# A two-layer linear-attention and MLP kernel: token pieces of the second joint stage dealt to other slots, and four steps of the joint pairs in another order

## The chip, the cores and the metric

The kernel runs on one core of one Trainium2 chip. The metric is the device time of one execution in microseconds. The engines are named as in the profile: PE (TensorE, the matmuls), DVE (VectorE), ACT (ScalarE), POOL (GpSimd) and SP (SyncE, which here issues the DMAs).

## The reference

The input is x, 2048 tokens of 448 numbers. Twice in turn it goes through an attention block and an MLP block, each added to its own input:

```python
    x = A_x
    x = x + _A_ref(_layernorm(x, axis=-1), A_wqkv, A_wo)
    x = x + _B_ref(_layernorm(x, axis=-1), B_w1, B_b1, B_w2, B_b2)
    x = x + _A_ref(_layernorm(x, axis=-1), A_wqkv, A_wo)
    x = x + _B_ref(_layernorm(x, axis=-1), B_w1, B_b1, B_w2, B_b2)
```

`_A_ref` is linear attention with 16 heads of 28. `_B_ref`, where the change lies, is `gelu(x @ w1 + b1) @ w2 + b2` with an inner width of 1792. All is float32.

## The kernel before, in words

**Arithmetic.** Each float32 operand of a matmul is held as two fp32r tiles, a high part (a cast on ACT) and a low part (the operand less its high part, on DVE). A product is made of three matmuls, high by high, low by high and high by low, so a matmul with a low part waits for a DVE subtraction. In the names an h or l at the end stands for these parts: `gh` and `gl` are the parts of a gelu's output, `XH` and `XL` those of the tokens.

**Blocks and slices.** The tokens are taken in four blocks of 512, the inner width in 14 slices of 128. A slice's first product (hp, hx, hy, hz) makes 128 x 512 values for a block, gelu follows on ACT, and `mlp2` (L1269) multiplies slice i of a block by w2 and adds it into four banks y, one for each 128 tokens: twelve matmuls of 448 columns. When a block's last slice is through, `mlp2` adds the banks to the block's rows on DVE (L1300, four operations) and SP stores them.

**Stages of a layer.** After attention, `classic` (L1407) does slices 0 to 9 of blocks 0 and 1 one by one. The two `joint` pairs (L1444, k = 0 and 1) do slices 10 to 13 for both blocks at once, and `eight` (L1553) does all seven pairs of slices for blocks 2 and 3. `joint` and `eight` use a Strassen-like scheme: `product(k)` (L1184) takes a pair of slices and two blocks through seven products with sums of weight pieces and of token pieces. Products 1, 6, 7 and 4 add up in one bank hx, 5 and 3 in hy, 2 in hz. `keep` (L1202) copies a state of hx or hy to s1, s2 or s5 on ACT, DVE adds another bank to it (L1474, L1478, L1502, L1507, L1603, L1616, L1622), and `high` and `low` make gelu, gh and gl of it. `later` makes only the gelu and puts it by. Since product 4 goes on adding in hx, it must wait until s5's addition has read that bank.

**Between the stages.** `remainder` (L1522) ends block 1 and begins with the gelus of block 0 that were put by; `LATER = (11, 10, 13, 12)` is the order of their slices and `divide` (L1243) makes their gh and gl. Slices 11 and 10 go through `mlp2` in `remainder`, 13 and 12 in the first pair of `eight`, and 12 is block 0's last.

**Token pieces.** Before `eight` the tokens of blocks 2 and 3 come as A11, A12, A21 and A22, and the sums S1 to S4 are made of them. `token_sum` (L1162) adds two pieces, the first half (128 x 512) on POOL and the second on DVE, both on line L1165. `token_piece` (L1167) makes the high part of a half on ACT (L1170) and the low part on DVE (L1171). Product 1 needs A11, 2 needs A12, 5 S1, 6 S2, 7 S3, 3 S4 and 4 A22. S2 is written over A11, S3 over A21 and S4 over A12, so a sum may only be made when the piece below it has been split.

**What sets the order.** The schedule is manual: an engine runs its instructions in the order in which the code writes them, and waits where a semaphore is missing. The table `PLAN` (L1319) lists by slot what `behind(l, i, tr)` writes at place i: "sS30" is `token_sum` S3, half 0, "tA121" is `token_piece` A12, half 1, and "y02" loads rows of block 0. Slots 24 and 25 stand in `remainder`, slot 27 in the first pair of `eight`, 28 in joint pair 0. Beside all this, `make` (L491) writes the next steps by which ACT, POOL and DVE prepare the weight pieces of a coming pair (`sevens`, L452; lines L431 to L486).

Of the kernel before, what the change touches and what calls it, by code (L numbers as in the profile page):

```python
# [12 lines left out]
OP = mybir.AluOpType  # L13
# [9 lines left out]
def linear_attn_mlp_kernel(  # L23
# [12 lines left out]
    pe, act, dve, pool, sp = nc.tensor, nc.scalar, nc.vector, nc.gpsimd, nc.sync  # L36
# [454 lines left out]
    def make(n, steps=1):  # L491
        if n < len(ahead):
            if n not in makers:
                makers[n] = (sevens if ahead[n][1] == "x" else chunks)(n)
            for _ in range(steps):
                next(makers[n], None)
# [31 lines left out]
    def stage_a(l, t):  # L528
        sts[l, t] = ln_stats(xt.pop((l, t)))
# [637 lines left out]
    def token_piece(l, name, h, eng=dve):  # L1167
        x = view(l, name, h)
        hi, lo = (cols(placed(l, k, name, h)) for k in range(2))
        act.copy(hi, x)  # L1170
        eng.tensor_tensor(lo, x, f(hi), op=OP.subtract)  # L1171
# [63 lines left out]
    def divide_high(g):  # L1235
        gh = t512("A", 2, "gh", F32R)
        act.copy(gh, g)  # L1237
        return gh, t512("B", 2, "gl", F32R, APART)

    def divide_low(g, gh, gl):  # L1240
        dve.tensor_sub(gl, g, f(gh))  # L1241

    def divide(i, g):  # L1243
        gs[i] = divide_high(g)
        divide_low(g, *gs[i])
# [64 lines left out]
    def load_part(l, t):  # L1310
# [86 lines left out]
    LATER = (11, 10, 13, 12)  # L1397
# [4 lines left out]
    def first_pair(l, b):  # L1402
        return l * (2 * NP + NC) + FIRST[b]

    came = {}
# [38 lines left out]
    def joint(l, k, tr):  # L1444

        n = first_pair(l, "j") + k
        p = NC + k
        c = Pair(l, 0, p, n)

        def step():  # L1450
            make(n + 1)

        c.product(1)
        s1 = c.keep(c.X, "s1")
        if k:
            step()
            c.product(5)
            s5 = c.keep(c.Y, "s5")
            c.product(2)
            dve.tensor_tensor(s1, s1, c.Z, op=OP.add)  # L1460
            step()
            mlp2(l, 1, 2 * p - 1)
            c.product(6)
            s2 = c.keep(c.X, "s2")
            c.high(s1, 0)
            c.low(0)
            step()
            make(n)
            make(n + 2)
            step()  # L1470
            behind(l, 22, tr)
            step()
            c.product(3)
            dve.tensor_tensor(s2, s2, c.Y, op=OP.add)  # L1474
            c.high(s2, 1)
            step()
            c.product(7)
            dve.tensor_tensor(s5, c.X, s5, op=OP.add)  # L1478
            c.low(1)
            c.later(s5, 1)  # L1480
            step()
        else:
            behind(l, 20, tr)
            step()
            c.product(2)
            dve.tensor_tensor(s1, s1, c.Z, op=OP.add)
            make(n + 2)
            c.product(5)
            s5 = c.keep(c.Y, "s5")
            behind(l, 30, tr)  # L1490
            c.product(6)
            s2 = c.keep(c.X, "s2")
            c.high(s1, 0)
            c.low(0)
            behind(l, 26, tr)
            step()
            step()
            mlp2(l, 1, CUT - 1)
            make(n)
            c.product(7)  # L1500
            step()
            dve.tensor_tensor(s5, c.X, s5, op=OP.add)  # L1502
            c.later(s5, 1)
            step()
            behind(l, 28, tr)
            c.product(3)
            dve.tensor_tensor(s2, s2, c.Y, op=OP.add)  # L1507
            c.high(s2, 1)
            c.low(1)
            step()  # L1510
            behind(l, 21, tr)
        mlp2(l, 1, 2 * p)
        if k:
            divide(LATER[0], came.pop(LATER[0]))
            behind(l, 23, tr)
        c.product(4)
        c.later(c.X, 0)
        step()
        if k == 0:
            step()  # L1520
# [32 lines left out]
    def eight(l, k):  # L1553

        n = first_pair(l, 2) + k
        c = Pair(l, 2, k, n)
        onward = k == NP - 1 and l + 1 < LAYERS

        def step():
            if k < NP - 1:  # L1560
                make(n + 1)

        c.product(1)
        s1 = c.keep(c.X, "s1")
        if k:
            step()
            c.product(5)
            s5 = c.keep(c.Y, "s5")
            step()
            if onward:  # L1570
                stage_a(l + 1, 0)
            c.product(2)
            dve.tensor_tensor(s1, s1, c.Z, op=OP.add)
            c.high(s1, 0)
            step()
            c.product(6)
            s2 = c.keep(c.X, "s2")
            make(n)
            if k < NP - 2:
                make(n + 2)  # L1580
            step()
            mlp2(l, 2, 2 * k - 1)
            c.low(0)
            step()
            c.product(3)
            dve.tensor_tensor(s2, s2, c.Y, op=OP.add)  # L1586
            c.high(s2, 1)
            step()
            c.product(7)
            dve.tensor_tensor(s5, c.X, s5, op=OP.add)  # L1590
            c.low(1)
            c.later(s5, 1)
            step()
            beside(l, k)
            if onward:
                stage_a(l + 1, 1)
        else:
            mlp2(l, 0, LATER[2])
            behind(l, 27, None)
            c.product(2)  # L1600
            make(n + 2)
            divide(LATER[3], came.pop(LATER[3]))
            dve.tensor_tensor(s1, s1, c.Z, op=OP.add)  # L1603
            c.product(5)
            s5 = c.keep(c.Y, "s5")
            c.product(6)
            s2 = c.keep(c.X, "s2")
            c.high(s1, 0)
            c.low(0)
            make(n)  # L1610
            mlp2(l, 0, LATER[3])
            step()
            step()
            step()
            c.product(7)
            dve.tensor_tensor(s5, c.X, s5, op=OP.add)  # L1616
            for h in range(2):
                token_piece(l, "A22", h)
            c.later(s5, 1)
            step()  # L1620
            c.product(3)
            dve.tensor_tensor(s2, s2, c.Y, op=OP.add)  # L1622
            step()
            c.high(s2, 1)
            c.low(1)
            step()
        mlp2(l, 2, 2 * k)
        c.product(4)
        c.later(c.X, 0)
        step()  # L1630
        if k == 0:
            step()
# [82 lines left out]
    for l in range(LAYERS):  # L1715
# [35 lines left out]
        for k in range(NP - NC):  # L1751
            joint(l, k, tr)
        remainder(l, tr)
        for k in range(NP):
            eight(l, k)
# [29 lines left out]
```

## Time and profile before

| | us |
|---|---|
| median of 3 runs | 876.27 (874.73 to 876.62) |
| the profiled execution's own time | 875.26 |
| its span, first to last instruction | 873.5 |
| PE busy in the span | 848.5 (97%) |
| DVE, ACT, POOL busy | 617.3, 515.7, 404.7 |

A row of the timeline has the start in us from the span's start, the duration, the engine, the line, what is written and from what, and in brackets how long the engine sat idle before it and who released it. Rows of one kind that follow one another are put together (x2, x4). Matmuls overlap: the start of one to the start of the next says more than a duration. The changed places come once in each layer: in the first layer between about 264 and 320 us, in the second between 693 and 751 us.

### The profile page before, as it was taken

What the parts mean: (1) busy time and instruction counts of PE and PEld (TensorE: products, weight loads), DVE (VectorE), ACT (ScalarE), POOL (GpSimd) and SP (SyncE); (2) the same over time, 40 slices, a digit from 0 to 9 for tenths busy, and PEclk for the clock granted to TensorE, in tenths of its full rate; (3) what the DMA queues carried; (4) which work ended last, traced back from release to release, by engine and by line L of the source; (5) the groups of instructions that cost most, each with busy time, mean ns of one, the idle gap of its engine ahead of it and who ended that gap; (6) DMA issues with size and microseconds to landing.
All of it is one profiled execution on the core that took longest, in us unless ns stands there. A gap on an engine that the chain in (4) does not pass through costs nothing.

```text
span 873.5 us, 12572 instructions
## 1 busy us (share of the span) xinstructions
PE 848.5 (97%) x4065; PEld 751.1 (86%) x4065; DVE 617.3 (71%) x1086; ACT 515.7 (59%) x1069; POOL 404.7 (46%) x474
## 2 busy tenths in 40 slices
PE   9999999999999899999999999989999998999998
PEld 8899987878888688889999998878888877888897
DVE  7898597568967775466888977953898669536443
ACT  7666664564676576664446665636556765665531
POOL 3456533455557544750533333243665582544310
PEclk9999999999999999999999999999999999999999
DMA  5375757656564533437545444584655453332361
GB/s 169 125 252 180 232 141 236 203 174 205 191 217 131 177 113 118 146 97 250 203 155 191 149 128 127 188 260 154 221 178 205 140 169 127 106 110 76 112 229 43
DMA packets 104461, 144.75 MB, mean 166 GB/s; under 512 B 10188, under 2 KB 91468, under 8 KB 104396
## 3 DMA queue, kind: packets, MB, share of 16 engines
q1 hardware_dynamic: 102620, 141.52, 49.4%
q10 hardware_dynamic: 1776, 2.44, 0.9%
q8 instruction: 32, 0.52, 0.3%
q14 instruction: 33, 0.27, 0.1%
HBM read 88.68 MB, written 50.86 MB: 160 GB/s over the span
## 4 chain that ended last, share of the span: by engine, by line
PE 60%; DVE 15%; ACT 8%; DMA 8%; issue 5%; POOL 2%; SPq 1%; DVEq 0%; ACTq 0%; POOLq 0%
PE hx L1200 9%; PE G L731 7%; PE psk L389 6%; PE y L1297 6%; PE y L1296 6%; PE y L1295 6%; PE psq L389 5%; PE hy L1200 4%; DMA temp<-in_B_w_dram 2%; PE hz L1200 2%; PE hp L1264 2%; DVE gl L1241 2%; DMA sp<-sq_q 2%; DVE pq L990 1%; ACT xm L1078 1%
## 5 line engine op out<-in xcount | busy, mean ns | idle before, releaser
L1297 PE MATMUL y<-w2h,gl 128*128 128x448 f32 x447 | 162.5, 363 | 7.8 <-DVE gl L1241 7.6
L1296 PE MATMUL y<-w2l,gh 128*128 128x448 f32 x447 | 164.3, 368 | 0.0
L1295 PE MATMUL y<-w2h,gh 128*128 128x448 f32 x447 | 163.4, 365 | 0.2 <-ACT gh L1237 0.2
L1241 DVE TENSOR_TENSOR gl<-g,gh 128x512 fp32r<-128x512 f32 x84 | 74.2, 883 | 68.8 <-ACT gh L1237 68.7
L1297 PEld LDWEIGHTS y<-w2h,gl 128*128 128x128 f32 x447 | 84.6, 189 | 17.1 <-DVE gl L1241 11.7
L1295 PEld LDWEIGHTS y<-w2h,gh 128*128 128x128 f32 x447 | 84.4, 189 | 9.9 <-ACT gh L1237 0.7
L1296 PEld LDWEIGHTS y<-w2l,gh 128*128 128x128 f32 x447 | 84.6, 189 | 6.5
L1264 PE MATMUL hp<-XH,W 128*128 128x512 f32 x280 | 87.8, 390 | 0.2 <-ACT XH L371 0.2
L1215 ACT ACTIVATE g<-s,b1s 128x256 f32<-128x256 f32 x84 | 38.2, 502 | 55.5 <-DVE s L1586 34.9
L1057 POOL TENSOR_TENSOR brs<-bst,few 128x1 f32<-128x1 f32 x32 | 18.2, 570 | 102.3 <-ACT bst L1055 102.3
L389 PE MATMUL psk<-wk,XH 128*128 128x448 f32 x210 | 61.8, 364 | 0.0
L570 POOL TENSOR_TENSOR xnl<-x,xnh 128x384 fp32r<-128x384 f32 x32 | 35.4, 1107 | 55.7 <-ACT xnh L569 27.8
L1264 PE MATMUL hp<-XL,W 128*128 128x512 f32 x160 | 60.7, 391 | 0.6 <-DVE XL L372 0.6
L1264 PEld LDWEIGHTS hp<-XH,W 128*128 128x128 f32 x280 | 52.4, 188 | 10.0 <-ACT XH L371 0.6
L389 PE MATMUL psq<-wq,XH 128*128 128x448 f32 x196 | 57.2, 365 | 0.3 <-DVE eq L408 0.3
L1237 ACT CAST gh<-g 128x512 fp32r<-128x512 f32 x84 | 52.1, 621 | 3.0 <-PE y L1296 0.6
L968 POOL TENSOR_TENSOR pz<-pq,zb 128x448 f32<-128x448 f32 x26 | 31.0, 1193 | 45.0 <-DVE dn L979 33.9
L1266 ACT ACTIVATE g<-hp,b1s 128x512 f32<-128x512 f32 x40 | 27.3, 682 | 36.9 <-PE hp L1264 27.7
L213 POOL TENSOR_TENSOR brs<-bve,few 128x1 f32<-128x1 f32 x31 | 17.1, 550 | 66.7 <-DVE bve L212 61.4
L731 PE MATMUL G<-kh,xnh 128*128 128x448 f32 x128 | 46.7, 368 | 0.0
L1200 PE MATMUL hx<-XH,W 128*128 128x512 f32 x140 | 43.7, 391 | 2.8 <-DVE s L1478 2.8
L731 PE MATMUL G<-kl,xnh 128*128 128x448 f32 x128 | 46.1, 365 | 0.2 <-DVE kl L618 0.2
(275 smaller groups left out, 2276.8 us busy)
## 6 DMA issues: line engine op xcount, KB each, us to landing
temp<-in_B_w_dram SPq DMA_DIRECT2D x20, 384.0 KB
x<-in_A_x_dram SPq DMA_DIRECT2D x32, 224.0 KB
pq_d<-eq SPq DMA_DIRECT2D x32, 224.0 KB
pq<-pq_d SPq DMA_DIRECT2D x32, 224.0 KB
g_d<-g SPq DMA_DIRECT2D x28, 256.0 KB
x<-x_d SPq DMA_DIRECT2D x32, 224.0 KB
gb<-g_d SPq DMA_DIRECT2D x28, 256.0 KB
raw<-in_B_w_dram SPq DMA_DIRECT2D x18, 384.0 KB
```

What stands on the lines that cost most here:

```text
L389: pe.matmul(o, x, p, start=(i == 0), stop=(i == 10))
L570: pool.tensor_tensor(lo[:, :TL], xn[:, :TL], f(h[:, :TL]), op=OP.subtract)
L731: pe.matmul(acc[c], w, k, start=first and c not in others[0], stop=last and c not in others[1])
L968: pool.tensor_tensor(pz, pq, tr.zb, op=OP.mult)
L1200: pe.matmul(o, w, r, start=(k in (1, 5, 2) and i == 0), stop=(i == len(made) - 1), skip_group_check=True)
L1215: act.activation(g[:, s].rearrange("p (u i n) -> p i u n", u=2, i=4), x[:, s].rearrange("p (i u n) -> p i u n", u=2, i=4), AF.Gelu_apprx_t ...
L1237: act.copy(gh, g)
L1241: dve.tensor_sub(gl, g, f(gh))
L1264: pe.matmul(hp, w, r, start=(k == 0), stop=(k == len(made) - 1))
L1295: pe.matmul(acc[j], gh[:, s], hi, start=first, stop=False)
L1296: pe.matmul(acc[j], gh[:, s], lo, start=False, stop=False)
L1297: pe.matmul(acc[j], gl[:, s], hi, start=False, stop=stop)
```

## The change

In the slots, seven entries go to a later slot and two sums go up within theirs:

```diff
-        "sS11 tA111 tA120 tA121 tS10 sS30 sS20 sS31",
+        "sS11 tA111 sS30 sS20 tA120",
...
-        "tS30 tS31 tS40 tS41",
+        "tS20 tS21 sS40 sS41 tS30 tS31 tS40 tS41",
```

Slot 25 is now "tA121 tS10 tS11 sS31 sS21" and the loads, where it was "tS11 sS21 tS20 tS21 sS40 sS41" and the loads. So the second half of A12, the first of S1 and a sum go from slot 24 to slot 25, and S2's pieces and S4's sums from 25 to 27.

In joint pair 1, the gelu of s2 and a step of the weights are written behind product 7 and s5's addition:

```diff
             c.product(3)
             dve.tensor_tensor(s2, s2, c.Y, op=OP.add)
-            c.high(s2, 1)
-            step()
             c.product(7)
             dve.tensor_tensor(s5, c.X, s5, op=OP.add)
+            c.high(s2, 1)
+            step()
             c.low(1)
```

In joint pair 0, `mlp2` of slice 10 of block 1 is written ahead of product 3 (it stood behind it, ahead of product 4):

```diff
             behind(l, 28, tr)
+            mlp2(l, 1, 2 * p)
             c.product(3)
...
-        mlp2(l, 1, 2 * p)
         if k:
+            mlp2(l, 1, 2 * p)
             divide(LATER[0], came.pop(LATER[0]))
```

In the first pair of `eight`, `divide` of slice 12 goes ahead of slot 27, and `mlp2` of slice 12, with the four additions of block 0's rows that it ends in, ahead of `low` of s1:

```diff
             mlp2(l, 0, LATER[2])
+            divide(LATER[3], came.pop(LATER[3]))
             behind(l, 27, None)
             c.product(2)
             make(n + 2)
-            divide(LATER[3], came.pop(LATER[3]))
             dve.tensor_tensor(s1, s1, c.Z, op=OP.add)
...
             c.high(s1, 0)
+            mlp2(l, 0, LATER[3])
             c.low(0)
             make(n)
-            mlp2(l, 0, LATER[3])
```

What this does to the engines' queues, all in the first layer: PE in joint pair 0, where product 3 (hy from S4) is taken out between product 7 (hx from S) and `mlp2` of slice 10:

```order
 L1200 MATMUL hx<-S_2837,W_130 128x512 x2
 L1200 MATMUL hx<-S_2838,W_130 128x512
-L1200 MATMUL hy<-S_3074,W_130 128x512 x2
-L1200 MATMUL hy<-S_3075,W_130 128x512
-L1200 MATMUL hy<-S_3074,W_130 128x512
-L1200 MATMUL hy<-S_3075,W_130 128x512
 L1295 MATMUL y_2371<-w2h,gh 128x448
 L1296 MATMUL y_2371<-w2l,gh 128x448
```

and put in behind that, right ahead of product 4 (hx from XH):

```order
 L1296 MATMUL y_2374<-w2l,gh 128x448
 L1297 MATMUL y_2374<-w2h,gl 128x448
+L1200 MATMUL hy<-S_3074,W_130 128x512 x2
+L1200 MATMUL hy<-S_3075,W_130 128x512
+L1200 MATMUL hy<-S_3074,W_130 128x512
+L1200 MATMUL hy<-S_3075,W_130 128x512
 L1200 MATMUL hx<-XH,W_130 128x512 x2
 L1200 MATMUL hx<-XL,W_130 128x512
```

Five matmuls went behind twelve. DVE in `remainder` before, from the second half of A11; the gl here is that of slice 13, and the L1165 rows are sums:

```order
L1171 TENSOR_TENSOR XL_129<-sp_3239,XH_128 128x2x256
L1171 TENSOR_TENSOR XL_129<-sp_3072,A12_3325 128x2x256
L1171 TENSOR_TENSOR XL_129<-sp_3239,A12_3325 128x2x256
L1171 TENSOR_TENSOR S1_3330<-S1_3286,XH_128 128x2x256
L1165 TENSOR_TENSOR sp_3241<-sp_3239,sp_3241 128x2x4x64
L1241 TENSOR_TENSOR gl_3354<-g_3266,gh_3352 128x512
```

and after, until gl of slice 12 (the second gl):

```order
L1171 TENSOR_TENSOR XL_129<-sp_3239,XH_128 128x2x256
L1171 TENSOR_TENSOR XL_129<-sp_3072,A12_3327 128x2x256
L1241 TENSOR_TENSOR gl_3348<-g_3266,gh_3346 128x512
L1171 TENSOR_TENSOR XL_129<-sp_3239,A12_3327 128x2x256
L1171 TENSOR_TENSOR S1_3352<-S1_3286,XH_128 128x2x256 x2
L1165 TENSOR_TENSOR sp_3241<-sp_3239,sp_3241 128x2x4x64
L1165 TENSOR_TENSOR sp_3239<-S1_3286,sp_3239 128x2x4x64
L1241 TENSOR_TENSOR gl_3402<-g_3293,gh_3400 128x512
```

gl of slice 13 has moved ahead of the second half of A12, the first half of S1 and a sum. DVE further on in the first pair of `eight`, before, from gl of slice 12 and s1's addition; the second gl is that of s1, slice 0 of blocks 2 and 3:

```order
L1241 TENSOR_TENSOR gl_3428<-g_3293,gh_3426 128x512
L1603 TENSOR_TENSOR s1_3394<-s1_3394,hz_3417 128x512
L1241 TENSOR_TENSOR gl_3453<-g_3448,gh_3451 128x512
L486 TENSOR_TENSOR W1_130<-raw_3046,W1_130 64x128
L1300 TENSOR_TENSOR r0_0_3367<-y0_3336,r0_0_3367 128x448
L1300 TENSOR_TENSOR r0_1_3369<-y1_3337,r0_1_3369 128x448
L1300 TENSOR_TENSOR r0_2_3371<-y2_3338,r0_2_3371 128x448
L1300 TENSOR_TENSOR r0_3_3373<-y3_3339,r0_3_3373 128x448
```

and after:

```order
L1604 TENSOR_TENSOR s1_3386<-s1_3386,hz_3421 128x512
L1300 TENSOR_TENSOR r0_0_3359<-y0_3330,r0_0_3359 128x448
L1300 TENSOR_TENSOR r0_1_3361<-y1_3331,r0_1_3361 128x448
L1300 TENSOR_TENSOR r0_2_3363<-y2_3332,r0_2_3363 128x448
L1300 TENSOR_TENSOR r0_3_3365<-y3_3333,r0_3_3365 128x448
L1241 TENSOR_TENSOR gl_3453<-g_3448,gh_3451 128x512
L486 TENSOR_TENSOR W1_130<-raw_3046,W1_130 64x128
```

The four additions of block 0's rows are now ahead of s1's gl. ACT's queue follows the same moves. PE's order in `eight`, the orders of POOL and SP, and every order in joint pair 1 stay as they were. L1478 is L1476 in the changed kernel, and lines from L1506 on are one higher.

More of the change, by code (lines that the diff above doesn't have):

```diff
@@ L1474, in joint @@
             dve.tensor_tensor(s2, s2, c.Y, op=OP.add)
+            c.product(7)
+            dve.tensor_tensor(s5, c.X, s5, op=OP.add)
             c.high(s2, 1)
             step()
-            c.product(7)
-            dve.tensor_tensor(s5, c.X, s5, op=OP.add)
             c.low(1)
```

2 rows, old and new, of the table PLAN are left out of this document.

## The prediction

> **What bounds the kernel now.** I read the page's busy times first, then TensorE's timeline around the places that the change touches, in both layers, then DVE, ACT and POOL there.
>
> ```profile
> PE 848.5 (97%) x4065; PEld 751.1 (86%) x4065; DVE 617.3 (71%) x1086; ACT 515.7 (59%) x1069; POOL 404.7 (46%) x474
> ```
>
> TensorE is busy for 848.5 of 873.5 us, so an edit can win only what PE waits for at its own place, or what a slow clock costs there. TensorE in the first layer, with the idle time before a row in brackets:
>
> ```profile
> 274.19 0.96 PE L1200 MATMUL hy<-S,W 128*128 128x512 f32 x3 [0.59 <-DVE S L1148]
> 274.98 0.37 PE L1295 MATMUL y<-w2h,gh 128*128 128x448 f32 x1
> ```
> ```profile
> 292.76 0.72 PE L1200 MATMUL hx<-XH,W 128*128 128x512 f32 x2 [1.38 <-DVE s L1478]
> ...
> 302.72 0.36 PE L1295 MATMUL y<-w2h,gh 128*128 128x448 f32 x1
> 302.92 0.37 PE L1296 MATMUL y<-w2l,gh 128*128 128x448 f32 x1
> 305.56 0.47 PE L1297 MATMUL y<-w2h,gl 128*128 128x448 f32 x1 [2.28 <-DVE gl L1241]
> ```
> ```profile
> 319.79 0.50 PE L1200 MATMUL hx<-XL,W 128*128 128x512 f32 x1 [0.33 <-DVE XL L1171]
> ```
>
> Four waits: product 3 of joint pair 0 (0.59), product 4 of joint pair 1 (1.38), the second product (mlp2) of slice 13 (2.28), product 4 of pair 0 of eight (0.33). All four end on DVE. The same four in the second layer:
>
> ```profile
> 703.80 0.97 PE L1200 MATMUL hy<-S,W 128*128 128x512 f32 x3 [1.39 <-DVE S L1148]
> ...
> 722.32 0.72 PE L1200 MATMUL hx<-XH,W 128*128 128x512 f32 x2 [1.38 <-DVE s L1478]
> ...
> 735.19 0.74 PE L1297 MATMUL y<-w2h,gl 128*128 128x448 f32 x1 [2.26 <-DVE gl L1241]
> ...
> 750.75 0.50 PE L1200 MATMUL hx<-XL,W 128*128 128x512 f32 x1 [0.23 <-DVE XL L1171]
> ```
>
> From product 4 of joint pair 1 to product 4 of eight it is 319.79 - 292.76 = 27.03 in the first layer and 750.75 - 722.32 = 28.43 in the second. The 1.40 between them is TensorE's clock, the third figure from the right in these rows of the stretches behind the two large gaps:
>
> ```profile
> 305.50:309.00 3.50, 3.44 (x16) 3.09 (x17) 3.42 (x7) 2.26 (x5) 0.00 (x0) 1.00 0.00 0
> 735.00:738.40 3.40, 3.21 (x9) 2.87 (x10) 3.32 (x7) 2.03 (x4) 0.00 (x0) 0.50 0.00 0
> ```
>
> Behind the gap of 2.26 us the granted clock was 0.50 for 3.4 us, behind the gap of 2.28 us it was 1.00: such a gap costs half clock sometimes. The Trainium skill ("TensorE: Matmul & The Clock Gate", Part 1) has the clock fall after at least one idle window of about 3.4 us, free-running. By that rule 2.26 us would be too short, and the second row says otherwise.
>
> **The change part by part.** Times are those of the first layer where no other is named.
>
> *Joint pair 1, the later gelu: nothing.* DVE ran s2's addition, then s5's, and ACT the gelu behind them, before and after; no engine's order differs there. Cost 0, and no cover is needed.
>
> *Joint pair 0, mlp2 of slice 10 ahead of product 3.* The matmul that waits for S could run without it at 274.19 - 0.59 = 273.60, and at 702.41. Now it comes behind twelve more, 2.4 later (0.20 each, 302.72 to 302.92): 276.0 and 704.8, when S is there since 274.19 and 703.80. Both waits go. Next late is product 4, which adds into the bank that s5's addition reads:
>
> ```profile
> 277.40 0.62 PE L1200 MATMUL hx<-XH,W 128*128 128x512 f32 x2
> ```
> ```profile
> 276.04 0.69 DVE L1502 TENSOR_TENSOR s<-hx,s 128x512 f32<-128x512 f32 x1
> ```
> ```profile
> 707.02 0.62 PE L1200 MATMUL hx<-XH,W 128*128 128x512 f32 x2
> ```
> ```profile
> 705.65 0.69 DVE L1502 TENSOR_TENSOR s<-hx,s 128x512 f32<-128x512 f32 x1
> ```
>
> DVE's queue ahead of this addition is as before, so it ends at 276.73 and 706.34. Product 4 starts 0.05 later, at 276.78 instead of 277.40 and at 706.39 instead of 707.02: 0.62 and 0.63 won in place of the whole waits.
>
> *What joint pair 1 makes of it.* Its product 4 waits for s5's addition there (L1478), which stands behind a weight subtraction that POOL holds up:
>
> ```profile
> 289.83 1.67 DVE L473 TENSOR_TENSOR W<-raw,W 128x512 fp32r<-128x512 f32 x1
> 291.43 0.67 DVE L1474 TENSOR_TENSOR s<-s,hy 128x512 f32<-128x512 f32 x1
> 292.02 0.68 DVE L1478 TENSOR_TENSOR s<-hx,s 128x512 f32<-128x512 f32 x1
> ```
> ```profile
> 288.59 1.06 POOL L470 TENSOR_TENSOR raw<-raw 128x256 f32<-128x256 f32 x1
> 289.61 1.34 POOL L1165 TENSOR_TENSOR S<-sp 128x512 f32<-128x512 f32 x1
> ```
>
> POOL's sum ends at 290.95 and the subtraction 0.55 later, at 291.50. POOL's times there do not hang on PE; DVE's do (product 6, copy, gelu, gh, gl) and come 0.62 earlier. L473 would be ready at 289.83 - 0.62 = 289.2, while L470 runs, and go in between L470 and the sum. Replayed, L473 is done at 290.5, s5's addition at 291.8, and product 4 starts there: 0.9 won, and 1.0 in the second layer, where all lies alike. Bounds: 0 (POOL's sum goes first again, 292.76 stays) and 1.0. I take 0.9 and 1.0, since L473 waited for the POOL operation that ran, no longer.
>
> *gl of slice 13 ahead of three DVE operations.* DVE and POOL before:
>
> ```profile
> 301.34 1.28 DVE L1171 TENSOR_TENSOR XL<-sp,A 128x512 fp32r<-128x512 f32 x2
> 302.54 1.76 DVE L1171 TENSOR_TENSOR S<-S,XH 128x512 fp32r<-128x512 f32 x1
> 304.23 0.68 DVE L1165 TENSOR_TENSOR sp<-sp 128x512 f32<-128x512 f32 x1
> 304.83 0.68 DVE L1241 TENSOR_TENSOR gl<-g,gh 128x512 fp32r<-128x512 f32 x1
> ```
> ```profile
> 302.45 1.30 POOL L1165 TENSOR_TENSOR sp<-sp 128x512 f32<-128x512 f32 x1 [2.19 <-DVE XL L1171]
> ```
>
> The changed queue has gl in the second place of that first pair: 301.94 to 302.62. The matmul that needs it comes at 302.72 + 2 x 0.20 = 303.12, so the gap of 2.28 is gone, with 0.5 to spare. The second half of A12 now meets POOL's sum (it ends at 303.75) and ends at 304.30, as S1's first half did. From there DVE goes on every 0.60: S1 until 305.5, the two sums, gl of slice 12 from 306.6, S2's halves until 308.5, then S3 and S4.
>
> TensorE meanwhile, with six matmuls of a product in 1.36 us and five in 1.13:
>
> ```profile
> 310.19 1.52 PE L1200 MATMUL hx<-S,W 128*128 128x512 f32 x6
> 311.55 0.36 PE L1295 MATMUL y<-w2h,gh 128*128 128x448 f32 x1
> ```
>
> mlp2 of slice 13 until 305.1, product 2 until 306.25, product 5 until 307.6. Product 6 needs S2's low halves at 308.06 and gets them at 308.56: a new wait of 0.5. mlp2 of slice 12 starts at 309.5 instead of 311.55, product 7 at 311.9, product 3 at 313.2, mlp2 of slice 0 at 314.4. This needs gl of slice 0, which now stands behind s1's addition and the four additions of block 0's rows:
>
> ```profile
> 311.62 0.68 DVE L1603 TENSOR_TENSOR s<-s,hz 128x512 f32<-128x512 f32 x1
> ```
> ```profile
> 314.97 2.22 DVE L1300 TENSOR_TENSOR r<-y,r 128x448 f32<-128x448 f32 x4
> ```
>
> DVE does as much ahead of s1's addition as it did, which so ends at 312.1 instead of 312.30. The rows follow until 314.25, gl until 314.9; PE needs it at 314.8: a wait of up to 0.2. Behind gl, where they were, the row additions would leave the four banks unread when mlp2 of slice 0 comes; ahead of it they cost gl 2.2, of which PE sees the 0.2.
>
> *Product 4 of eight* needs the low halves of A22, here with POOL beside them:
>
> ```profile
> 317.91 1.83 DVE L1171 TENSOR_TENSOR XL<-sp,A 128x512 fp32r<-128x512 f32 x2
> ```
> ```profile
> 316.32 0.74 POOL L432 TENSOR_TENSOR W<-raw,W 128x256 fp32r<-128x256 f32 x1
> 317.15 0.84 POOL L466 TENSOR_TENSOR raw<-raw 128x256 f32<-128x256 f32 x1
> 318.07 1.12 POOL L467 TENSOR_TENSOR raw<-raw 128x256 f32<-128x256 f32 x1
> ```
>
> These POOL operations hang on s1's addition through ACT, so they come 0.2 earlier. Before, the A22 pair came 0.7 behind the rows (317.19 to 317.91); now it comes 0.7 behind gl (314.9), with an estimated 0.6 for a weight piece of POOL's that a copy between them waits for. So it is ready at 316.2, meets L432 (until 316.9) and L466, and ends at about 318.65. PE, which is there at 317.46, goes on at 318.7 instead of 319.79: 1.1 won, with a new wait of 1.2. Bounds: 2.33 if POOL is never in the way, 0 if L467 too goes ahead of the second half. I take 1.1, where the two engines take turns as in these rows. The Trainium skill ("SBUF — State Buffer", SBUF: two separate sides) calls the port pair of these two engines an exclusive lock held for a whole instruction; 1.76 beside POOL against 0.68 alone agrees. It speaks against this change, which moves DVE work to where POOL runs its chain.
>
> *Sum.* First layer 0.9 + 1.1 = 2.0. Second layer 1.0 + 1.1 + 1.4 of clock, as no gap of 2 us is left there = 3.5. The timeline has no wait of PE behind product 4 in the rest of eight, so 5.5 stays won. The profiled execution took 875.26 (span 873.5 and 1.76 around it), 1.0 below the median of 876.27, and the sum is made against it: 869.8. The clock can put single runs 1.4 apart.
>
> **The rivals.**
>
> *POOL keeps joint pair 1 where it is.* For: POOL does not follow PE there. Against: L473 would be ready before the sum. Nothing of 1.9: 871.7. Chance 0.17.
>
> *The half clock is not the gap's.* For: one gap of 2.3 us had none. It then falls elsewhere, and 1.4 is not won: 871.2. Chance 0.08. The page on the clock gate, by its window of 3.4 us, would have it so.
>
> *The wait only moves.* A22's low halves stay at 319.74, PE waits 2.3 at product 4, and both layers get half clock there: 869.8 + 2 x 1.1 + 2 x 1.4 = 874.8. For: DVE, with hardly an idle moment from 295 to 312, is the bound. Against: before, all that stands ahead of A22 waited with the rows for mlp2 of slice 12, and this now comes 2 us earlier. Chance 0.07.
>
> *Slower: POOL runs its whole chain ahead of A22.* If L432, L466, L467 and the two behind them run without a break, at about 0.8 each until 320.1, A22 ends at 321.25: 1.5 later than before, with a PE gap of 3.8 and half clock behind it in both layers. That is 2 x 2.6 + 2 x 1.4 over the forecast: 877.8. It decides from about 320 on, where the gap is 2.5. Against: 1.83 for the pair shows that POOL let DVE in between. Chance 0.06.
>
> **How the numbers follow.** Forecast 869.8, chance 0.62. Low end 867.3: A22 without POOL (2 x 1.2). High end 873.4: nothing won at A22 (2 x 1.1) and one half clock more (1.4), which takes in the first two rivals. No change is within 0.2% (1.75 us, about what a measurement of this kernel can tell): 874.5 to 878.0. Faster 0.62 + 0.17 + 0.08 = 0.87, same 0.07, slower 0.06.
>
> **What would show it.** Right: no wait at mlp2 of slice 13 and no clock of 0.50 behind it, product 4 of joint pair 0 waiting for s5's addition (0.3 and 1.1), new waits at product 6 (0.5) and at product 4 of eight (about 1.2). Wrong: a wait of over 2 us at product 4 of eight, L473 ending with POOL's sum again, or a wait still at mlp2 of slice 13.

## The result, and the profile after

The changed kernel took 871.85 us (median of 5 runs, 870.01 to 873.98), the kernel before 876.27 (874.73 to 877.48): a ratio of 0.995, 95% interval 0.9929 to 0.9972, or 4.4 us. The profiled execution is the one of 871.85, 3.4 below that of before (875.26). The forecast was 869.8 (867.3 to 873.4). Faster was right and the range held the time, but the joint part of the gain mostly failed, as the text's first rival had it. That 871.85 lies so near the 871.7 of that rival is chance (see the section on the prediction).

PE on the page of the changed kernel is as busy as before, in a span that is 3.4 shorter (870.1):

```profile
PE 849.1 (98%) x4065; PEld 747.7 (86%) x4065; DVE 618.7 (71%) x1086; ACT 515.6 (59%) x1069; POOL 404.8 (47%) x474
```

PE's timeline of the changed kernel at the four places, first layer:

```profile
275.09 1.29 PE L1200 MATMUL hy<-S,W 128*128 128x512 f32 x5
276.47 0.74 PE L1200 MATMUL hx<-XH,W 128*128 128x512 f32 x2
...
292.46 0.73 PE L1200 MATMUL hx<-XH,W 128*128 128x512 f32 x2 [1.35 <-DVE s L1476]
...
302.82 0.36 PE L1297 MATMUL y<-w2h,gl 128*128 128x448 f32 x1
...
308.42 1.21 PE L1200 MATMUL hx<-S,W 128*128 128x512 f32 x4 [0.43 <-DVE S L1171]
...
318.66 0.50 PE L1200 MATMUL hx<-XL,W 128*128 128x512 f32 x1 [0.94 <-DVE XL L1171]
```

The same in the second layer:

```profile
703.58 1.29 PE L1200 MATMUL hy<-S,W 128*128 128x512 f32 x5
704.97 0.73 PE L1200 MATMUL hx<-XH,W 128*128 128x512 f32 x2
...
719.87 0.72 PE L1200 MATMUL hx<-XH,W 128*128 128x512 f32 x2 [0.89 <-DVE s L1476]
...
746.08 0.50 PE L1200 MATMUL hx<-XL,W 128*128 128x512 f32 x1 [0.94 <-DVE XL L1171]
```

Product 3 (hy from S) no longer waits, the second product of slice 13 (302.82) has no gap, and small waits have come at product 6 (0.43) and product 4 of eight (0.94). But product 4 of joint pair 1 still waits 1.35 in the first layer: from product 4 of joint pair 0 to this one it now takes 292.46 - 276.47 = 15.99 instead of 15.36. What was won at the first is lost at the second. In the second layer it is 14.90 instead of 15.30.

The joint pairs of the two layers differ by some ten nanoseconds in which engine starts first. DVE in the changed kernel, first layer:

```profile
287.49 1.28 DVE L1241 TENSOR_TENSOR gl<-g,gh 128x512 fp32r<-128x512 f32 x1 [3.02 <-ACT gh L1237]
288.80 0.71 DVE L486 TENSOR_TENSOR W<-raw,W 64x128 fp32r<-64x128 f32 x1
289.54 1.67 DVE L473 TENSOR_TENSOR W<-raw,W 128x512 fp32r<-128x512 f32 x1
```

POOL beside it:

```profile
287.48 0.74 POOL L469 TENSOR_TENSOR raw<-raw 128x256 f32<-128x256 f32 x1
288.30 1.06 POOL L470 TENSOR_TENSOR raw<-raw 128x256 f32<-128x256 f32 x1
289.32 1.34 POOL L1165 TENSOR_TENSOR S<-sp 128x512 f32<-128x512 f32 x1
```

DVE in the second layer:

```profile
715.96 0.69 DVE L1241 TENSOR_TENSOR gl<-g,gh 128x512 fp32r<-128x512 f32 x1 [3.00 <-ACT gh L1237]
...
717.43 1.18 DVE L473 TENSOR_TENSOR W<-raw,W 128x512 fp32r<-128x512 f32 x1
```

POOL in the second layer:

```profile
715.96 1.29 POOL L469 TENSOR_TENSOR raw<-raw 128x256 f32<-128x256 f32 x1
717.33 0.74 POOL L470 TENSOR_TENSOR raw<-raw 128x256 f32<-128x256 f32 x1
718.03 1.72 POOL L1165 TENSOR_TENSOR S<-sp 128x512 f32<-128x512 f32 x1
```

In the first layer POOL's L469 starts at 287.48 and gl at 287.49; gl takes 1.28, and so L473 comes behind the sum. In the second layer both start at 715.96 (5 ns apart, too little for these rows to tell which was first), gl takes 0.69 and POOL's operation 1.29; L473 goes in ahead of the sum, and it is the sum that is long.

From product 4 of joint pair 1 to product 4 of eight it is 318.66 - 292.46 = 26.20 instead of 27.03 in the first layer, and 26.21 instead of 28.43 in the second, where the granted clock is now full (third figure from the right, about where it was 0.50 before; over the whole span it is 1.000):

```profile
733.00:736.40 3.40, 3.00 (x13) 2.10 (x12) 3.37 (x7) 2.18 (x4) 0.00 (x0) 1.00 0.00 0
```

### The profile page after: what moved, and what is told of

Read it like the earlier page. It is cut to its first block, busy times and chain, and to the rows that moved or that the text cites. A ratio compares the mean times of both kernels' runs of the same rounds, so it can differ in the third digit from the quotient of the medians.

```text
span 870.1 us, 12570 instructions
## 1 busy us (share of the span) xinstructions
PE 849.1 (98%) x4065; PEld 747.7 (86%) x4065; DVE 618.7 (71%) x1086; ACT 515.6 (59%) x1069; POOL 404.8 (47%) x474
```

## The experiments

All twelve runs stand beside the kernel before, which took 875.6 to 876.0 (90 runs in four series); the changed kernel first had five runs, e7, e8 and e9 have six each, e6 one, the others 11 or 12. One view serves them all, the starts of the same matmuls of PE in each profile. J0 is from the start of the joint stage to product 4 of joint pair 0, J1 from there to product 4 of joint pair 1, E0 from there to product 4 of pair 0 of eight, in us; the two figures are the two layers, from unrounded starts. The last two columns are from all timed runs: the mean time not granted by the clock (one less the granted clock, times the span) and the ratio to before.

| kernel | J0 | J1 | E0 | not granted | ratio (95%) |
|---|---|---|---|---|---|
| before | 13.39, 14.22 | 15.36, 15.29 | 27.04, 28.44 | 3.07 | 1 |
| before again (e6) | 13.44, 13.31 | 15.31, 15.43 | 27.36, 28.00 | | |
| changed | 12.76, 12.76 | 15.99, 14.90 | 26.19, 26.21 | 1.28 (with e5) | 0.995 (0.9929 to 0.9972) |
| changed again (e5) | 13.23, 12.76 | 15.91, 15.97 | 26.20, 27.33 | | 0.995 (0.9934 to 0.9966) |
| e1 joint alone | 12.76, 13.39 | 14.90, 15.89 | 27.12, 27.27 | 2.84 | 0.9996 (0.9981 to 1.0011) |
| e2 eight alone | 13.40, 13.77 | 15.35, 15.31 | 26.20, 27.33 | 1.09 | 0.9976 (0.9964 to 0.9987) |
| e3 slots alone | 13.73, 13.80 | 15.26, 15.31 | 28.21, 28.31 | 3.35 | 0.9999 (0.9986 to 1.0013) |
| e11 no slots | 13.37, 13.44 | 15.36, 15.33 | 26.57, 27.66 | 3.20 | 0.9997 (0.9982 to 1.0012) |
| e12 joint and sum | 12.76, 12.76 | 14.99, 14.88 | 28.56, 27.04 | 3.85 | 0.998 (0.9963 to 0.9996) |
| e4 sum later | 12.76, 13.75 | 14.99, 14.91 | 27.42, 26.95 | 1.19 | 0.9968 (0.9955 to 0.998) |
| e7 sum on DVE | 12.78, 12.76 | 15.01, 14.88 | 26.21, 26.19 | 0.43 | 0.9931 (0.9908 to 0.9954) |
| e8 A22 early | 12.76, 13.30 | 15.99, 15.88 | 25.78, 26.70 | 0.87 | 0.9926 (0.9902 to 0.995) |
| e9 sum and A22 | 12.76, 12.76 | 14.98, 14.88 | 25.54, 25.56 | 1.16 | 0.9935 (0.9917 to 0.9952) |
| e10 rows behind | 12.76, 12.76 | 15.98, 15.97 | 27.18, 27.95 | 1.35 | 0.9965 (0.9953 to 0.9977) |

E0 holds a third meeting of DVE and POOL, in `remainder`, and with it the largest differences between layers. DVE and POOL in e5, second layer, at gl of slice 11, and PE behind them:

```profile
723.79 1.80 DVE L1241 TENSOR_TENSOR gl<-g,gh 128x512 fp32r<-128x512 f32 x1 [0.32 <-ACT gh L1237]
```
```profile
723.75 1.30 POOL L1165 TENSOR_TENSOR sp<-sp 128x512 f32<-128x512 f32 x1
```
```profile
726.27 0.44 PE L1295 MATMUL y<-w2h,gh 128*128 128x448 f32 x1 [0.96 <-DVE r L1300]
```

The same gl in the changed kernel's first profile, where that sum starts only at 723.18:

```profile
722.21 0.69 DVE L1241 TENSOR_TENSOR gl<-g,gh 128x512 fp32r<-128x512 f32 x1 [0.32 <-ACT gh L1237]
```

With gl late, block 1's row additions are late, and PE waits 0.8 to 1.0 for a bank. This is so in seven second layers (e6, e5, e2, e3, e8, e10, e11), with either kernel's order, and in none with POOL's sum in joint pair 1 done by DVE (e7, e9, e12). Cut at the first matmul of `eight`, its part up to product 4 is alike in all layers of a kernel: 18.4 to 18.5 in before, e6 and e1 (19.8 with half clock in it), 17.5 to 17.7 with the eight part (changed, e5, e2, e4, e7), 16.9 in e8 and e9. So the eight part wins about 0.85 there in every layer, whatever E0 shows.

**e1, the joint edit alone.** The kernel before with one edit:

```diff
             behind(l, 28, tr)
+            mlp2(l, 1, 2 * p)
             c.product(3)
...
-        mlp2(l, 1, 2 * p)
         if k:
+            mlp2(l, 1, 2 * p)
```

> The kernel before with one edit of the change: in joint pair 0 the second product of slice 10 stands ahead of product 3. Theory (each gain is made and lost where DVE and POOL meet): the waits for S at product 3 (0.59 and 1.39) go, product 4 of joint pair 0 comes 0.6 earlier in both layers, and product 4 of joint pair 1 comes 0 to 1.0 earlier, according to which of gl of joint pair 1 and POOL's operation takes the port pair first; the gap of 2.3 at the second product of slice 13 stays in both layers. Time 0 to 1.8 below the kernel before. Rival (the joint edit carries the measured 4.4 through what it makes later): 3 or more below. Rival (POOL holds joint pair 1 whatever PE does): product 4 of joint pair 1 at the same place as before in both layers, time within 0.5 of before.

875.35, between 1.7 below the kernel before and 1.0 above it. In the first layer DVE got in and the pair came to 12.76 + 14.90; in the second to 13.39 + 15.89, as long as before. The gap stays in both layers (2.35 and 2.23), and so does the loss of clock. The first rival is out; the edit alone is worth too little to see.

**e2, the eight part alone**, which is the change without the edits to the two joint pairs:

```diff
-        "sS11 tA111 tA120 tA121 tS10 sS30 sS20 sS31",
+        "sS11 tA111 sS30 sS20 tA120",
...
+            divide(LATER[3], came.pop(LATER[3]))
             behind(l, 27, None)
...
+            mlp2(l, 0, LATER[3])
             c.low(0)
```

> The kernel before with the edits to the token pieces' slots, to the division of slice 12 and to the place of the second product of slice 12, without the joint edits. Theory: joint pairs as before (waits 0.59 and 1.39 at product 3, 1.38 at product 4 of joint pair 1), the gap at slice 13 gone, product 4 of pair 0 of eight 0.8 earlier than before in each layer, and 1.4 more wherever the execution before has half clock behind the gap: 1.6 to 3.4 below the kernel before, about 3.0. Rival (the eight part only moves its wait to product 4 of eight and the gain is the joint part's): within 0.8 of before. Rival (half clock comes whatever the gaps): windows of half clock in this profile too, 1.6 below.

873.27, 1.1 to 3.2 below. E0 is 26.20 in the first layer, as in the whole change, and 27.33 in the second, by the wait in `remainder`; the gap at slice 13 is gone, and the clock not granted falls from 3.07 to 1.09.

**e3 and e11, halves of the eight part.** e3 has the new slots without the moved division and second product, e11 has those two without the slots.

> The kernel before with the token pieces' slots of the change alone; the division of slice 12 stays behind the pieces of its slot and the second product of slice 12 stays where it was. Theory (DVE's queue decides): the gap of 2.3 at slice 13 goes, but gl of slice 12 now stands behind six more pieces, ends near 311.2 in the first layer where PE wants it at 309.9, and a new gap of 1.0 to 1.7 opens there; product 4 of eight 0 to 0.5 earlier per layer: 0 to 1 below before, and up to 1.4 to 2.8 more if the half clock goes with the gap of 2.3. Rival (the slots alone carry the gain, the moved division is worth nothing): as the eight part whole, 1.6 to 3.4 below, without a gap of over 0.5 at slice 12.

PE in e3, first layer, at the second product of slice 12:

```profile
310.98 0.47 PE L1295 MATMUL y<-w2h,gh 128*128 128x448 f32 x1 [0.68 <-ACT gh L1237]
312.72 0.48 PE L1297 MATMUL y<-w2h,gl 128*128 128x448 f32 x1 [1.06 <-DVE gl L1241]
```

875.21, no gain: the gap went from slice 13 to slice 12 in two pieces (0.68 and 1.06), both in one stretch of the clock's grid (below), with half clock behind them in the first layer.

> The kernel before with the division of slice 12 ahead of its slot and with the second product of slice 12 ahead of the low half of s1, without the new slots and without the joint edits. Theory (the pieces ahead of gl of slice 13 make the gap): the gap of 2.2 to 2.4 stays in both layers and with it the half clock in some executions (1.2 to 1.9 windows of 3.413 us in an execution on average, as in the kernel before); time within 0.8 of the kernel before. Rival (the division and the row additions carry the eight part): 1.5 to 3 below the kernel before.

875.39, no gain either: the gap at slice 13 is there in both layers (2.26 and 2.27), and the clock not granted stays at 3.20. (`eight` up to product 4 is 0.5 shorter, 17.9, but pair 1 gives back 0.3 and 0.8.) So neither half wins alone. The slots take the pieces from in front of gl of slice 13, and the moved division keeps them from standing in front of gl of slice 12.

**e10, the row additions behind gl again.** The changed kernel with this undone:

```diff
-            mlp2(l, 0, LATER[3])
             c.low(0)
             make(n)
+            mlp2(l, 0, LATER[3])
```

> The changed kernel with the second product of slice 12 of block 0, and with it the four row additions, behind the low half of s1 again, where it was before (and without the edit to joint pair 1, which moves no instruction). Theory (the row additions fill the time in which DVE would wait for ACT, and read the banks that slice 0 of block 2 needs): behind gl and a weight piece the rows end 1 to 2 later, the second product of slice 0 waits 0.5 to 1.0 for its first bank, and product 4 of eight comes 0.3 to 0.8 later: 0.6 to 1.6 above the changed kernel. Rival (the place of the rows is worth nothing, PE waits at product 4 anyway): within 0.3 of the changed kernel.

PE in e10, first layer:

```profile
315.13 0.44 PE L1295 MATMUL y<-w2h,gh 128*128 128x448 f32 x1 [0.90 <-DVE r L1300]
...
319.17 0.51 PE L1200 MATMUL hx<-XL,W 128*128 128x512 f32 x1 [0.92 <-DVE XL L1171]
```

871.92, 0.7 above the changed kernel's second measurement, with intervals that overlap (0.9953 to 0.9977 against 0.9934 to 0.9966). In the profile it is plain: slice 0 waits 0.90 for a bank that L1300 has not read, and `eight` up to product 4 takes 18.4 in both layers instead of 17.6, the upper end of the 0.3 to 0.8 that had been expected and as long as in the kernel before. (E0 shows 1.0 in the first layer; 0.2 of it lies in `remainder`.)

**e4, POOL's sum one slot later.** The changed kernel with

```diff
-        "sS10",
-        "sS11 tA111 sS30 sS20 tA120",
+        "",
+        "sS10 sS11 tA111 sS30 sS20 tA120",
```

> The changed kernel with POOL's sum for S1 (first half) dealt from the slot in joint pair 1 to the next, ahead of the pieces that stand there. Theory (the term of the joint part was lost at the weight subtraction of joint pair 1, which waits for this sum): the subtraction takes about 0.7 instead of 1.67 and 1.18, and product 4 of joint pair 1 comes 0.9 earlier in the first layer and 0.5 in the second: 1.4 below the changed kernel, if what follows keeps it. Rival (POOL's weight operation ahead of the sum holds the subtraction): no change at that product, time within 0.3 of the changed kernel. Rival (the sum is late for the pieces of S1 and S2): a wait of over 1 at product 6 or product 2 of pair 0 of eight, time the same or 1 above the changed kernel.

PE in e4, first layer:

```profile
292.22 0.72 PE L1200 MATMUL hx<-XH,W 128*128 128x512 f32 x2 [0.40 <-DVE s L1476]
...
299.86 0.47 PE L1297 MATMUL y<-w2h,gl 128*128 128x448 f32 x1 [0.87 <-DVE gl L1241]
```

The sum does hold the subtraction: with it away the wait at product 4 is 0.40 and J1 is 14.99 and 14.91. But POOL now runs three sums in a row beside DVE, gl of slice 10 takes 1.77, and E0 is 27.42 and 26.95; what is lost lies in `remainder`, since `eight` up to product 4 takes 17.7, against 17.6 in the changed kernel. 872.72: the meeting was moved, not removed. The place of the loss had been expected at products 6 and 2 and came earlier.

**e7, the sum on DVE.** The changed kernel with POOL's sum taken out and, in joint pair 1,

```diff
             step()
+            token_sum(l, "S1", 0, dve)
             c.low(1)
```

> The changed kernel with the first half of S1's sum done by DVE, behind s5's addition in joint pair 1, where DVE stood idle for 0.84, instead of by POOL. Theory (the joint part's term was lost because POOL's sum held the weight subtraction; moving the sum on POOL only moved the meeting): the subtraction takes 0.7, product 4 of joint pair 1 comes 14.9 to 15.0 behind that of joint pair 0 in both layers, and the eight stage takes 26.2 as in the changed kernel: 1.0 below it in the first layer, 0 to 0.9 in the second, 1 to 2 in all. Rival (DVE is so full that its sum pushes the chain of token pieces as POOL's did): eight 0.6 to 1.2 longer, time as the changed kernel.

DVE in e7, first layer:

```profile
290.25 0.69 DVE L473 TENSOR_TENSOR W<-raw,W 128x512 fp32r<-128x512 f32 x1
...
292.06 0.68 DVE L1165 TENSOR_TENSOR S<-sp 128x512 f32<-128x512 f32 x1
292.99 0.69 DVE L1241 TENSOR_TENSOR gl<-g,gh 128x512 fp32r<-128x512 f32 x1 [0.24 <-ACT gh L1237]
```

870.04, 1.2 below the changed kernel's second measurement (intervals overlap: 0.9908 to 0.9954 against 0.9934 to 0.9966), and all segments as expected: J1 15.01 and 14.88, E0 26.21 and 26.19. The sum takes 0.68 where POOL took 1.34, in time in which DVE stood idle. The six runs also lost 0.85 less to the clock than the changed kernel's (0.43 against 1.28), so the gain rests on the segments more than on the time. The Trainium skill ("SBUF — State Buffer", SBUF: two separate sides) calls the port pair of these engines an exclusive lock; 0.69 for L473 without POOL's sum and 1.67 behind it agree.

**e12, the joint edit with the sum on DVE**, on the kernel before and without the eight part: the edits of e1 and e7 together.

> The kernel before with the second product of slice 10 ahead of product 3 in joint pair 0 (the joint edit alone) and with the first half of S1's sum on DVE behind s5's addition in joint pair 1; no eight edits. Theory (the joint edit's gain of 0.6 is real and is given back only where POOL's sum holds the weight subtraction): product 4 of joint pair 0 comes 12.8 behind the joint stage's start and product 4 of joint pair 1 14.9 to 15.0 behind that, in both layers, 27.7 in place of 28.75 and 28.7 to 29.5; the gap of 2.3 at slice 13 and 1.4 to 1.9 windows of half clock in an execution stay: 1.6 to 3.0 below the kernel before, against 0.4 for the joint edit alone. Rival (DVE's chain of token pieces takes the time back, through a wider gap at slice 13): product 4 of eight 0.7 to 1.0 later after product 4 of joint pair 1 than before, time within 0.8 of the kernel before.

873.93, 0.35 to 3.2 below, where e1 was within 1.7 of no change. J0 and J1 together are 27.75 and 27.64, so the two edits win at least 1.0 in each layer (28.75 and 29.51 in before, 28.75 and 28.74 in e6). J0, which ends ahead of the sum, is 12.76 in both layers: that 0.6 is the joint edit's, and joint pair 1 no longer takes it back. No run has the sum on DVE without the joint edit, so whether the other 0.4 needs both is not shown. Its two gaps at slice 13 also show the clock (last section).

**e8 and e9, A22 earlier.** e8 is the changed kernel with, in pair 0 of eight,

```diff
+            for h in range(2):
+                token_piece(l, "A22", h)
             c.high(s1, 0)
-            mlp2(l, 0, LATER[3])
-            c.low(0)
+            mlp2(l, 0, LATER[3], lambda: c.low(0))
             make(n)
+            c.product(7)
+            dve.tensor_tensor(s5, c.X, s5, op=OP.add)
             step()
             step()
             step()
-            c.product(7)
-            dve.tensor_tensor(s5, c.X, s5, op=OP.add)
-            for h in range(2):
-                token_piece(l, "A22", h)
```

(the lambda puts gl between the first and the second row addition).

> The changed kernel with the low and high halves of A22 ahead of the gelu of s1 in pair 0 of eight, the row additions of block 0 around gl of slice 0 (one ahead, three behind), and s5's addition ahead of two weight steps. Theory (product 4 of eight waits 0.94 because the A22 pair, 1.81 instead of 1.2, and two weight pieces in front of it share the ports with POOL's weight chain): the pair now runs while POOL is idle, in 1.2 to 1.3, the wait at product 4 goes to 0 to 0.3, product 4 comes 0.6 to 0.9 earlier in each layer; 1 to 1.9 below the changed kernel, less what waits for ACT in pair 1 of eight. Rival (DVE's length of work decides, not the meeting): s5's addition ends where A22 ended, product 4 waits 0.9 as before. Rival (gl of slice 0 is late): a wait of 0.5 to 1.2 at the second product of slice 0 in place of that at product 4, time the same.

DVE in the changed kernel ahead of product 4 of eight:

```profile
314.73 0.72 DVE L486 TENSOR_TENSOR W<-raw,W 64x128 fp32r<-64x128 f32 x1
315.48 0.79 DVE L464 COPY raw<-W 128x256 f32<-128x256 f32 x1
316.19 0.68 DVE L1617 TENSOR_TENSOR s<-hx,s 128x512 f32<-128x512 f32 x1
316.79 1.81 DVE L1171 TENSOR_TENSOR XL<-sp,A 128x512 fp32r<-128x512 f32 x2
```

DVE in e8:

```profile
311.39 1.29 DVE L1171 TENSOR_TENSOR XL<-sp,A 128x512 fp32r<-128x512 f32 x2
...
315.70 0.29 DVE L486 TENSOR_TENSOR W<-raw,W 64x128 fp32r<-64x128 f32 x1
316.02 0.69 DVE L1615 TENSOR_TENSOR s<-hx,s 128x512 f32<-128x512 f32 x1
316.62 0.28 DVE L464 COPY raw<-W 128x256 f32<-128x256 f32 x1
```

The weight loads of PE in e8:

```profile
314.12 0.19 PEld L1297 LDWEIGHTS y<-w2h,gl 128*128 128x128 f32 x1 [0.23 <-DVE gl L1241]
314.66 0.19 PEld L1295 LDWEIGHTS y<-w2h,gh 128*128 128x128 f32 x1 [0.35 <-DVE r L1300]
316.76 0.30 PEld L1200 LDWEIGHTS hx<-A,W 128*128 128x128 f32 x2 [0.40 <-DVE s L1615]
319.75 0.19 PEld L1200 LDWEIGHTS hy<-XH,W 128*128 128x128 f32 x1 [0.36 <-DVE W L473]
```

869.42, 1.8 below the changed kernel's second measurement, again with overlapping intervals. The meeting is gone: the same three kinds of work take 0.29, 0.28 and 1.29 instead of 0.72, 0.79 and 1.81. The run changes three places at once, so it does not part what the shorter work won from what the new order won. `eight` up to product 4 takes 16.9 instead of 17.6 in both layers, 0.7 less, as expected (E0 shows 0.4 in the first layer, because `remainder` took 0.2 longer). PE now waits a little for gl, for a bank and for s5's addition, and product 5 of the next pair then waits for its weights (L473): pair 1 of `eight` gives back another 0.4 and 0.6.

> The changed kernel with both: the first half of S1's sum on DVE in joint pair 1, and A22 ahead of the gelu of s1 in pair 0 of eight. Theory (two separate meetings of DVE and POOL, one in each stage): product 4 of joint pair 1 comes 14.9 to 15.0 behind that of joint pair 0 as with the sum alone, and product 4 of eight 25.8 behind that as with A22 alone in the first layer; the two gains add less what pair 1 of eight gives back at its weights (0.4): 868.0 to 869.8. Rival (the sum's place is taken from what hides A22): the eight stage takes 26.2 or more again, time as either alone, 869.4 to 870.1 or more.

869.31: J1 is that of e7, and E0 is shorter than in e8 (25.54 and 25.56) because `remainder` has no wait; `eight` up to product 4 is 16.9 as in e8. But the time (0.9917 to 0.9952) does not part from either alone. The best of these versions are some 6 us below the kernel before.

**e5 and e6, both kernels once more.**

> The changed kernel once more, for a narrower interval and a second profile. In the six profiles so far the half clock (3.413 us at 0.50, from the ends of a grid of 3.413 us that each execution starts at another point) followed every grid window in which TensorE was idle for 1.69 us or more, and no window with 1.66 or less. Theory (the gaps of 2.3 bring it by where they fall on the grid): the changed kernel has no wait of over 1.4 at the places of the change, so no half clock between 264 and 560 or after 692; half clock can come near 158 and 586, where the change does nothing. Median 871.5 to 873.0. Rival (half clock by chance): half clock in the stretches of the change too. Product 4 of joint pair 1 in the first layer comes 15.0 or 16.0 behind that of joint pair 0, according to which of gl and POOL's operation starts first. The matmuls of the rest stage follow each other every 200 ns or every 204 ns in each layer.

> The kernel before once more, for a second profile. Theory: gaps of 2.2 to 2.4 at the second product of slice 13 in both layers again; half clock behind each of them exactly where a window of the grid holds 1.69 us or more of idle TensorE, by the phase of this execution. Rival: half clock where no window holds so much, or none where one does. If the pace of 204 ns in the rest stage belongs to the change, this profile shows 200 ns in both layers; if it is an accident of the execution, 204 ns may stand here too.

The changed kernel took 871.19 (12 runs) beside 875.77, the kernel before 874.17 in its single run. e6 had both gaps (2.29 and 2.27) and half clock behind neither. What e5 foresaw of the clock held at the places of the change, not to the hundredth elsewhere (last section).

## Why the prediction was right, and where it failed

*Waits for S: right.* Both are gone, in every profile with this order, and product 4 of joint pair 0 comes at 276.47, 0.93 earlier, of which the stage's earlier start made 0.30; 0.63 against 0.62. It starts 0.05 behind the end of s5's addition, as foreseen: 1.38 behind the start of product 3, whose five matmuls take 1.13, a wait of 0.25 (forecast 0.3). In the second layer J0 fell by 1.46 and not by 0.63, since before's profile had 14.22 there; e6 has 13.31, so most of this belongs to that execution: one of S's subtractions on DVE (L1148) took 1.64 there, beside POOL, and 0.68 after. In four of eighteen layers with this order (one each in e1, e4, e5 and e8) it took 1.64 or 1.65 too, and product 4 waited 0.6 to 1.1 for s5's addition.

*Joint pair 1: this step failed.* "L473 would be ready at 289.83 - 0.62 = 289.2, while L470 runs, and go in between L470 and the sum." The replay moved gl 0.62 earlier and kept its 0.82. In the changed order it starts within 0.12 of POOL's L469, and where POOL is first by 7 ns or more, gl takes 1.17 to 1.28 and L473 is ready behind the sum's start. Of the ten joint pairs with this order and POOL's sum in place (changed, e5, e1, e8, e10), J1 was 15.9 to 16.0 in eight and 14.90 in two; the ten with the old order have 15.26 to 15.43. So the forecast's 0.9 and 1.0 were 0 or less in eight of ten pairs, which is the first rival, given 0.17. Its reason, that POOL does not follow PE, was right: in the first layer the sum starts 25.60 behind the joint stage's start in before (289.61 - 264.01) and 25.61 after (289.32 - 263.71), while PE came 0.63 earlier. That this sum does the holding is shown too: without it on POOL, J1 is 14.88 to 15.01 in all six pairs of e7, e9 and e12.

*Gap at slice 13: right.* The gap is gone, product 6 waits 0.43 (forecast 0.5), slice 0 shows no wait of note. e11 shows that the slots are needed for it, e3 that without the two other moves the gap goes to slice 12, and e10 that without the moved row additions slice 0 waits instead.

*Product 4 of eight: right in kind, 0.3 too much.* 0.83 was won instead of 1.1, with a wait of 0.94 instead of 1.2. The text allowed 0.6 for one weight piece ahead of A22; there were two, of 0.72 and 0.79, and A22 was ready at 316.79 instead of 316.2.

*"So 5.5 stays won": wrong by 0.9.* By PE's starts, pair 1 of eight gave back 0.3 in the first layer and 0.6 in the second. PE came earlier and met ACT's copies, which had been in time:

```profile
756.13 0.74 PE L1200 MATMUL hx<-XH,W 128*128 128x512 f32 x2 [0.30 <-ACT s L1204]
```

*The 1.4 of clock: right in size on the average, by more chance than the text said.* It was read off one execution. In the profiles without the new slots (before, e6, e1, e11, e12) there are ten such gaps, and half clock followed two. Over all timed runs, though, the clock not granted fell from 3.07 (90 runs) to 1.28 (17 runs). A half-clock stretch of 3.41 holds back 1.71 by this count and cost 28.43 - 27.03 = 1.40, so 1.79 is worth an estimated 1.5. The three kernels that keep the gap at slice 13 (e1, e11, e12) have 3.30 on average, the six others without it 1.07; e3, which moves it to slice 12, has 3.35. So the rival by which the 1.4 is not won is out. The timed runs show only a mean clock, so where the lost clock lay is open: in the five profiles with the gap only two of ten half-clock stretches follow the gap, the other eight lie near 160 and 587 us and at the end, where the eight profiles without it (e3 left out) have six.

*The two last rivals* are out: product 4 waited 0.94, not over 2.

*The number.* Between the two profiles the second layer won 1.85 in J0 and J1, against an execution of before that was slow there, 0.9 in `eight` and 1.3 of clock; the first won 0.3 ahead of the joint stage, nothing in J0 and J1 together, and 0.8 in `eight`. Pair 1 of `eight` gave back 0.9, and the rest stage lost 1.4 by its pace (last section). Several of these have nothing to do with the forecast's terms, so the time's place in the range is partly luck.

*What stays open.* e2 is 1.1 to 3.2 below before, e1 is between 1.7 below and 1.0 above, and the whole (second measurement) 3.0 to 5.8 below. By the middles that is 2.5 for the parts and 4.4 for the whole; the intervals allow both that they add up and that they do not.

## What to carry to other kernels

Where two engines hold each other up, do not replay one of them with the durations of before: ask which operation of the other starts within its shift, and price both orders. A sum that met another engine's chain was here best given to an engine that stood idle at that place; moved along its own queue, it met something else. An idle stretch of PE costs its length and, if it leaves PE idle for over about half of one stretch of the clock's grid (next section), half clock on top; two of ten gaps of 2.3 us did, and e3's two waits of 0.68 and 1.06 in one stretch did as well, so the pieces of a split gap must lie apart.

## What the runs showed that was not expected

**The clock's grid.** The half-clock stretches are 3.413 us long and lie whole multiples of 3.413 from each other: in before they start at 588.187 and 734.960, 43 apart, in e3 at 159.464, 313.064 and 589.544, 45 and 81 apart. Where the grid starts differs between executions. A stretch is at half clock when PE was idle for about half of the one ahead of it. At slice 13 the two gaps with half clock behind them left PE idle for 2.03 and 1.88 within one stretch of the grid, the eight others for 1.70 or less, since the grid cut them in two. Granted clock in e12 behind a gap of 2.29 and behind one of 2.28:

```profile
306.30:309.60 3.30, 3.30 (x10) 2.69 (x9) 3.21 (x6) 3.30 (x7) 0.00 (x0) 0.50 0.00 0
733.00:736.30 3.30, 1.63 (x8) 1.53 (x9) 3.30 (x6) 0.45 (x1) 0.00 (x0) 1.00 0.00 0
736.30:739.70 3.40, 3.40 (x17) 2.89 (x16) 3.31 (x7) 3.40 (x8) 0.00 (x0) 1.00 0.00 0
```

Near 157 and 583 us and at the end both outcomes occur from 1.5 to 1.8; the ends of matmuls are modelled in a profile, so these sums are not exact. The Trainium skill ("TensorE: Matmul & The Clock Gate", Part 1) has the clock fall after an idle window of about 3.4 us; here half of one did it, on a grid that runs free as that part says.

**Two paces of the same matmuls.** In the rest stage, behind `eight` (from about 402 us in the first layer), PE runs triples of 448-column matmuls for 30 to 40 us without a wait, every 200 or every 204 ns on average, and keeps the pace that it fell into at the stage's start: 0.7 us for a layer. PE (first figures) in the changed kernel:

```profile
406.00:426.00 20.00, 20.00 (x99) 18.37 (x99) 14.79 (x28) 7.59 (x13) 3.84 (x5) 1.00 0.95 328
840.00:860.00 20.00, 20.00 (x99) 18.38 (x98) 6.70 (x9) 4.98 (x8) 5.29 (x4) 1.00 0.28 106
```

PE in e6, the kernel before once more:

```profile
406.00:426.00 20.00, 20.00 (x99) 18.39 (x98) 14.78 (x28) 7.59 (x13) 3.84 (x5) 1.00 0.94 324
840.00:860.00 20.00, 20.00 (x102) 18.76 (x101) 6.11 (x9) 5.44 (x9) 5.37 (x4) 1.00 0.43 149
```

99 matmuls in 20 us or 102, in either kernel, so this is not the change's. It did take 1.4 from what the first two profiles differ by, as before's had the quick pace in both layers. What sets the pace was not found.
